# When the last weights are converted, and where copies and joins stand, at the seam between two FFNs

## The chip, the cores and the metric

The kernel runs on one core of a Trainium2 chip. Its engines are TensorE (PE in the profile; PEld is its weight load), VectorE (DVE), ScalarE (ACT), GpSimd (POOL) and SyncE (SP, which issues the DMAs). Each engine works through its own instructions in the order in which the program gives them; semaphores hold an instruction until what it needs is there. The metric is the device time of one execution in microseconds; less is better.

## The reference

Three stages run one after the other on 1536 tokens of width 512:

```
x   = attention(q, k, v)           # 16 heads, banded (|i-j| < 16) plus 24 block summaries
h   = x @ w_in                     # 512 -> 2048        first FFN
x   = (h * cos(h)) @ w_out         # 2048 -> 512
h   = x @ w_in2                    # 512 -> 1024        second FFN
e   = exp(h - max(h));  solu = h * e / (sum(e) + 1e-9)
ln  = (solu - mean) / sqrt(var + 1e-6) * g_ln
out = ln @ w_out2                  # 1024 -> 512
```

All is 32-bit in effect; the weights arrive as 64-bit floats.

## The kernel before

**Products.** A 32-bit product is made of three on PE: each operand is split into a high part (rounded by ScalarE to the format that PE takes) and a low part (the operand less its high part), and high x high, high x low and low x high are summed in PSUM (PASSES, L218). Every operand so needs a rounding and a subtraction before PE can use it.

**Weights.** The class Weights (L111) takes one block of 128 x 512 weights at a time through stages: `load` fetches the 64-bit words (tag raw, three buffers), `rebias` lets ScalarE convert both words (L164, L165), `finish` lets VectorE join them to 32-bit floats (L172, tag s, three buffers, or b, two), and for the second FFN's last weights w_out2 lets GpSimd multiply by the column g_ln (L179); `split` rounds on ScalarE (L194) and subtracts on GpSimd (L195). `turn` does one round of all stages, each for another block.

**First FFN.** 48 steps (NSTEP), each 12 products h (L245) and 12 products y (L287). `emit_chain` (L997) puts the work of the other engines for one step in order: ScalarE's u (L254), the weights' split and rebias, VectorE's n (L259), the join, gs (L274, L275), the sine (L264), r (L269). Up to four banks of y are added to X by VectorE (`evacuate`, L301). A step so converts one block of weights beside the products.

**The second FFN's first product** uses seven block products in place of eight (p = a pair of token tiles). The blocks of W and X are formed as sums: `w2_blocks` (L741) gets four blocks m1, n1, n2, m2 for each of two halves c, and forms differences of them on GpSimd (`less`, L745) and splits the seven (`w2_tile`, L735: ScalarE L737, GpSimd L738). All this is done when the block's turn comes in `split`, inside one step of the first FFN. For X, `sum_xo` (L809, GpSimd) and `split_xo` (L827) do the same for a pair.

**The seam** is written out by hand after the loop (from L1057): the last step of the first FFN, the pair 0 of the second (its products on the first FFN's spare banks), with `weights.turn()` six times for the last six blocks of w_out2, each between parts of pair 0 and pair 1. `emit_block` (L878) sums banks and takes maxima, `emit_exp2`, `emit_mult2`, `emit_stats`, `emit_factors` and `emit_scaled` make the normalised tile e; `emit_factors` ends in a power on GpSimd (L930) for which `emit_scaled` (L935) waits. Tile t = 0 is turned by PE (`turn`); later tiles by DMA: `emit_planes` (L978) separates the halves of the words, a DMA transposes them, `emit_join` (L984) puts them together on ScalarE (L991, into a buffer of tag s), rounds (L994) and subtracts on GpSimd (L995). `emit_o2` is the last product, `emit_out` copies it (L1028) and writes it.

**Loop over pairs** (L1135). For p > 1 the products m = 1, 6, 7, 5 go to four banks; m = 2 uses the bank of m = 1 again, so PE waits until ScalarE has copied it (`emit_p1`, L862), which stands behind `emit_planes(s - 2)` on ScalarE. The sums of X for the pair p + 2 take two of the three buffers s that the joins use too.

Of the kernel before, what the change touches and what calls it, by code (L numbers as in the profile page):

```python
# [34 lines left out]
def fused_kernel(  # L35
# [75 lines left out]
    class Weights:  # L111
# [5 lines left out]
        def __init__(self):  # L117
            self.jobs = []
            self.raw = {}
            self.f32 = {}  # L120
            self.done = {}
            self.next = 0
            self.queue = []
            self.ready = []
            self.limit = 0
# [15 lines left out]

        def bits(self):
# [6 lines left out]
            for n in range(i, i + 2):  # L149
                self.load(n)  # L150
            self.f32[i] = conv.tile([P, 512], I32, tag="b" if self.jobs[i][6] else "s", name="s",
                                    bufs=2 if self.jobs[i][6] else 3) if wide else self.raw[i]

        def rebias(self):

            if self.queue and wide:
                t = self.raw[self.queue[-1]]
                hw, lw = as32(t[:, :, 1]), t[:, :, 0]
                nc.scalar.activation(out=hw, in_=hw, func=AF.Prelu, scale=REBIAS, alpha=NEGATIVE)  # L164
                nc.scalar.activation(out=lw, in_=lw.bitcast(U32), func=AF.Copy, scale=TOP3)  # L165

        def finish(self):

            if self.queue and wide:
                i = self.queue[-1]  # L170
                t = self.raw[i]
                nc.vector.scalar_tensor_tensor(  # L172
                    out=self.f32[i], in0=t[:, :, 1], scalar=3, in1=t[:, :, 0],
                    op0=ALU.logical_shift_left, op1=ALU.bitwise_or)
            for i in self.queue:
                scale = self.jobs[i][4]
                if scale is not None:
                    f = as32(self.f32[i]) if wide else self.f32[i]
                    nc.gpsimd.tensor_scalar(out=f, in0=f, scalar1=scale, scalar2=None, op0=ALU.mult)  # L179
            self.ready = self.queue  # L180
            self.queue = []

        def split(self):

            for i in self.ready:
                f = self.f32.pop(i)
                f = as32(f) if wide else f
                pool, scale, then = self.jobs[i][3:6]
                if then is not None:
                    then(f)  # L190
                    self.done[i] = None
                    continue
                w = pool.tile([P, 2, 512], F32R, tag="w", name="w")
                nc.scalar.activation(out=w[:, 0, :], in_=f, func=AF.Copy)  # L194
                nc.gpsimd.tensor_tensor(out=w[:, 1, :], in0=f, in1=as32(w[:, 0, :]), op=ALU.subtract)  # L195
                self.done[i] = w
            self.ready = []
# [505 lines left out]
    with tc.manual_schedule():  # L703
# [37 lines left out]
        def w2_blocks(c):  # L741
# [4 lines left out]

            def m1(t):
# [37 lines left out]
        B_DONE, C_DONE, A_DONE = (GF * NTB * g for g in (2, 3, 4))  # L785
        ALLOWED = {B_DONE: W2O - KC, C_DONE - 2: W2O + 2, NSTEP - 3: W2O + NF2}

        def split_next(step):
# [3 lines left out]
            for p, which in XO_AT.get(step, ()):  # L792
                if 0 in which:
                    sum_xo(p)
                split_xo(p, which, nc.scalar)

# [7 lines left out]
                 NSTEP - 3: ((1, (1,)),), NSTEP - 2: ((1, (2,)),), NSTEP - 1: ((1, (3,)),)}  # L804

# [258 lines left out]
        emit_m(0, 1, 6, 7)  # L1064
        emit_u(L)
        emit_n(L)
        split_next(L)
        emit_sin(L)
        emit_r(L)
        emit_g(L)  # L1070
        emit_p1(0)
        table(AF.Exp)
        banks_of[0].append(h_tile(NSTEP + 3))
        emit_u2(0)
        emit_u3(0)
        emit_m(0, 5)
        weights.turn()
# [5 lines left out]
        weights.turn()  # L1083
# [5 lines left out]
        weights.turn()  # L1089
# [7 lines left out]
        weights.turn()  # L1097
# [11 lines left out]
        weights.turn()  # L1109
        emit_p1(1)  # L1110
        emit_u2(1)
        weights.turn()
# [22 lines left out]
        for p in range(1, NPT):  # L1135
# [18 lines left out]
            for k, o in enumerate(outs):  # L1154
                emit_o2(o, O[2 + k] if p == 1 else O[k])
# [7 lines left out]
            if p == 1:  # L1163
                emit_planes(1)
                emit_out(0)
# [4 lines left out]
            if p < NPT - 1:  # L1170
                emit_planes(f)
            emit_stats(s)
# [5 lines left out]
            if p == 1:  # L1178
                emit_join(1)
            else:  # L1180
# [57 lines left out]
```

## Time and profile before

| | |
|---|---|
| median of 3 runs | 525.38 us (524.36 to 527.4) |
| the profiled execution | 523.5 us, its span 521.7 us, mean granted clock 0.97 |
| PE busy | 478.4 us, 92% of the span |
| DVE, ACT, POOL busy | 309.3, 319.2, 239.9 us |
| chain that ended last, share by engine | PE 65%, DVE 8%, POOL 7%, ACT 6% |

The page gives the busy share of each engine in 40 slices of 13.04 us. PE is the engine with the most work; where its digit is under 9 it waits for another, and the waits view says for which. The timeline then shows what that engine was doing. A bracket at the end of a timeline row, as [3.92 <-ACT gs], is the idle time ahead of the instruction and what ended it.

### The profile page before, as it was taken

To read this page: it belongs to the slowest core of one execution; us is meant where nothing else is said; L and a number is where in the kernel's file an instruction comes from. 1 tells how busy PE (TensorE), PEld (TensorE's weight loads), DVE (VectorE), ACT (ScalarE), POOL (GpSimd) and SP (SyncE) were. 2 spreads that over 40 slices of the span, in tenths; PEclk is the share of its full clock that TensorE was granted. 3 is DMA by queue.
4 is the path that set the end of the run, shared out by engine and by line. 5 is a ranking of instruction groups with operands and counts; after the bars stand their busy time and mean duration, and the time that the engine had idled before them with its cause. 6 is when DMAs were issued, how large, how long until landed. Compare 5 with 4: busy or idle time off the path is not lost.

```text
span 521.7 us, 8063 instructions
## 1 busy us (share of the span) xinstructions
PE 478.4 (92%) x2907; PEld 390.9 (75%) x2907; DVE 309.3 (59%) x744; ACT 319.2 (61%) x566; POOL 239.9 (46%) x236
## 2 busy tenths in 40 slices
PE   8999999999999999999969969999778269999997
PEld 5777777688888888888858858888557158888886
DVE  4888576745444566465625534545687557967840
ACT  3688787747766656656544546437434377878731
POOL 3679787323221222212352255543556566785310
PEclk9999999999999999999999988999979769999999
DMA  8889854002323233232210222001200413142111
GB/s 242 254 223 221 210 141 134 1 1 93 110 82 119 82 92 111 82 109 93 84 69 8 91 70 83 0 1 40 82 1 0 101 41 91 51 103 80 42 60 42
DMA packets 59048, 46.18 MB, mean 89 GB/s; under 512 B 40448, under 2 KB 51328, under 8 KB 59008
## 3 DMA queue, kind: packets, MB, share of 16 engines
q1 hardware_dynamic: 59008, 45.67, 30.4%
q8 instruction: 23, 0.38, 0.3%
q14 instruction: 17, 0.14, 0.1%
HBM read 36.61 MB, written 3.15 MB: 76 GB/s over the span
## 4 chain that ended last, share of the span: by engine, by line
PE 65%; DVE 8%; POOL 7%; ACT 6%; issue 5%; DMA 4%; SPq 3%; POOLq 0%; DVEq 0%; ACTq 0%
PE y L287 22%; PE h L245 21%; PE h L1018 12%; PE h L854 7%; DMA vt<-in_v_dram 2%; SPq L413 2%; POOL w L738 1%; POOL s L745 1%; ACT raw L164 1%; PE sps L530 1%; DMA vt<-vm 1%; DVE s L172 1%; POOL w L195 1%; ACT raw L165 1%; POOL sm L545 1%
## 5 line engine op out<-in xcount | busy, mean ns | idle before, releaser
L287 PE MATMUL y<-gs,w 128*128 128x512 f32 x576 | 142.9, 398 | 8.4 <-ACT gs L274 7.8
L245 PE MATMUL h<-xs,w 128*128 128x512 f32 x576 | 141.3, 392 | 0.0
L287 PEld LDWEIGHTS y<-gs,w 128*128 128x128 f32 x576 | 110.6, 192 | 33.2 <-ACT gs L274 8.7
L245 PEld LDWEIGHTS h<-xs,w 128*128 128x128 f32 x576 | 107.4, 188 | 21.8
L195 POOL TENSOR_TENSOR w<-s,w 128x512 fp32r<-128x512 f32 x40 | 52.0, 1301 | 116.3 <-ACT w L194 110.7
L854 PE MATMUL h<-w,xo 128*128 128x512 f32 x252 | 62.8, 408 | 21.1 <-ACT p L862 14.2
L254 ACT ACTIVATE r<-h 128x512 int32<-128x512 f32 x48 | 28.6, 596 | 86.9 <-PE h L245 86.9
L172 DVE SCALAR_TENSOR_TENSOR s<-raw 128x512 int32<-128x512 int32 x48 | 36.8, 767 | 67.7 <-ACT raw L165 62.4
L259 DVE SCALAR_TENSOR_TENSOR r<-r,h 128x512 f32<-128x512 int32 x48 | 32.9, 686 | 73.6 <-ACT r L254 73.4
L854 PEld LDWEIGHTS h<-w,xo 128*128 128x128 f32 x252 | 49.7, 199 | 32.9 <-ACT p L862 14.6
L1018 PE MATMUL h<-w,ls 128*128 128x512 f32 (+1 forms) x312 | 67.0, 373 | 0.0
L1018 PEld LDWEIGHTS h<-w,ls 128*128 128x128 f32 x312 | 55.3, 188 | 10.2
L264 ACT ACTIVATE r<-r,half_pi 128x512 f32<-128x512 f32 x48 | 34.5, 719 | 5.1 <-DVE r L259 5.1
L269 DVE TENSOR_TENSOR h<-h,r 128x512 f32<-128x512 f32 x48 | 33.0, 688 | 5.6 <-ACT r L264 5.6
L738 POOL TENSOR_TENSOR w<-s,w 128x512 fp32r<-128x512 f32 x14 | 18.0, 1288 | 38.7 <-ACT w L737 38.7
L275 DVE TENSOR_TENSOR gs<-h,gs 128x512 fp32r<-128x512 f32 x48 | 32.7, 680 | 4.7 <-ACT gs L274 4.7
L194 ACT ACTIVATE w<-s 128x512 fp32r<-128x512 f32 x40 | 25.0, 626 | 12.4 <-POOL s L179 12.4
L164 ACT ACTIVATE raw<-raw 128x512 f32<-128x512 f32 x48 | 31.9, 665 | 0.0
L165 ACT ACTIVATE raw<-raw 128x512 int32<-128x512 uint32 x48 | 31.9, 664 | 0.0
L995 POOL TENSOR_TENSOR ls<-s,ls 128x512 fp32r<-128x512 f32 x18 | 23.3, 1293 | 17.8 <-ACT ls L994 17.8
L991 ACT ACTIVATE s<-turned 128x1024 uint16<-128x1024 uint16 x18 | 24.6, 1366 | 7.4 <-POOL xo L842 7.4
L274 ACT ACTIVATE gs<-h 128x512 fp32r<-128x512 f32 x48 | 28.2, 587 | 1.5 <-DVE h L269 1.5
(102 smaller groups left out, 671.0 us busy)
## 6 DMA issues: line engine op xcount, KB each, us to landing
raw<-in_moe_w_in_dram SPq DMA_DIRECT2D x24, 512.0 KB, 3.7
raw<-in_moe_w_out_dram SPq DMA_DIRECT2D x24, 512.0 KB, 3.5
vt<-in_v_dram SPq DMA_DIRECT2D x16, 240.0 KB, 5.7
kt<-in_k_dram SPq DMA_DIRECT2D x8, 384.0 KB, 5.2
qt<-in_q_dram SPq DMA_DIRECT2D x8, 384.0 KB, 7.1
out_dram<-osb SPq DMA_DIRECT2D x11, 256.0 KB, 2.0
vt<-vm SPq DMA_DIRECT2D x16, 72.0 KB
vt<-in_v_dram SPq DMA_DIRECT2D x16, 48.0 KB, 6.4
```

What stands on the lines that cost most here:

```text
L164: nc.scalar.activation(out=hw, in_=hw, func=AF.Prelu, scale=REBIAS, alpha=NEGATIVE)
L165: nc.scalar.activation(out=lw, in_=lw.bitcast(U32), func=AF.Copy, scale=TOP3)
L172: nc.vector.scalar_tensor_tensor(out=self.f32[i], in0=t[:, :, 1], scalar=3, in1=t[:, :, 0], op0=ALU.logical_shift_left, op1=ALU.bitwise_or)
L195: nc.gpsimd.tensor_tensor(out=w[:, 1, :], in0=f, in1=as32(w[:, 0, :]), op=ALU.subtract)
L245: nc.tensor.matmul(h, lhsT=w[:, a, f * P:(f + 1) * P], rhs=xs_of[tb, c][:, b_, :], start=(m == 0), stop=(m == 3 * KC - 1))
L259: nc.vector.scalar_tensor_tensor(out=r, in0=r.bitcast(I32), scalar=TWO_PI, in1=h_of[step], op0=ALU.mult, op1=ALU.subtract)
L264: nc.scalar.activation(out=r, in_=r, func=AF.Sin, scale=-1.0, bias=half_pi)
L269: nc.vector.tensor_tensor(out=h, in0=h, in1=r, op=ALU.mult)
L275: nc.vector.tensor_tensor(out=gs[:, 1, :], in0=r, in1=as32(gs[:, 0, :]), op=ALU.subtract)
L287: nc.tensor.matmul(y[e], lhsT=w[:, a, e * P:(e + 1) * P], rhs=gs[:, b_, :], start=(f == 0 and i == 0), stop=(f == GF - 1 and i == 2))
L854: nc.tensor.matmul(banks_of[p][BANK[m]], lhsT=x[:, a, s0:s0 + P], rhs=w2_of[m, c][:, b_, :], start=c == j == 0, stop=c == 1 and j == 2)
L1018: nc.tensor.matmul(o, lhsT=ls_of[t][f // 4][:, a, s0:s0 + P], rhs=w[:, b_, cols], start=(f == 0 and i == 0), stop=(f == NF2 - 1 and i == 2))
```

## The change

Four things are altered; the products on PE are the same and in the same order.

1. **W's sums and splits.** The split of a block that is a sum is put off to the next step (`split_later`), and one of the subtractions (n2 less n1) moves from the step of n2 to that of m2.
2. **The last product's weights.** GpSimd's multiplication by g_ln is gone: ScalarE rounds with the scale, and VectorE forms the low part as w x g less the high part (`low_one`), where GpSimd subtracted before. The stages can be called one by one; blocks 0 and 1 go through the loop some steps later than before, blocks 2 to 7 by hand, with conversion (`rebias`), join, high part and low part at separate places.
3. **X's sums** for pairs 0 and 1 are formed a step earlier.
4. **At the seam**, the second set of e products stands before u of pair 1; the first output is copied before the planes of tile 1, and uses the fourth bank instead of the third; the join of tile 1 stands before the statistics of tile 3 and so before the sums of X for pair 3.

```diff
+        def low_one(self, i):
+            f, scale = self.low.pop(i)
+            w = self.done[i]
+            nc.vector.scalar_tensor_tensor(
+                out=w[:, 1, :], in0=f, scalar=scale, in1=as32(w[:, 0, :]), op0=ALU.mult, op1=ALU.subtract)
...
-            for i in self.queue:
-                scale = self.jobs[i][4]
-                if scale is not None:
-                    f = as32(self.f32[i]) if wide else self.f32[i]
-                    nc.gpsimd.tensor_scalar(out=f, in0=f, scalar1=scale, scalar2=None, op0=ALU.mult)
...
         def split(self):
+            later, self.later = self.later, []
+            for do in later:
+                do()
...
             def n1(t):
                 f["n1"] = t
                 less("m1", "n1", "m1")
-                w2_tile((5, c), f["m1"])
+                split_later((5, "m1"))
 
             def n2(t):
                 f["n2"] = t
                 w2_tile((3, c), t)
                 less("m1", "n2", "m1")
-                w2_tile((6, c), f["m1"])
-                less("n2", "n2", "n1")
-                w2_tile((7, c), f["n2"])
+                split_later((6, "m1"))
 
             def m2(t):
                 f["m2"] = t
                 w2_tile((2, c), t)
+                less("n2", "n2", "n1")
                 less("m2", "m2", "m1")
-                w2_tile((4, c), f["m2"])
+                split_later((7, "n2"), (4, "m2"))
...
+        XO_SUM = {NSTEP - 7: 0, NSTEP - 5: 1}
+        LOAD = {NSTEP - 6: (3,), NSTEP - 5: (4,), NSTEP - 2: (5,), NSTEP - 1: (6,)}
+        REBIAS_AT = {NSTEP - 3: (2,), NSTEP - 2: (3, 4)}
+        JOIN_AT = {NSTEP - 3: (2,), NSTEP - 2: (3,)}
...
         emit_u2(0)
+        high(4)
+        rebias(5)
+        rebias(6)
         emit_u3(0)
+        low(4)
+        join(5)
+        high(5)
         emit_m(0, 5)
-        weights.turn()
...
         emit_exp2(1)
-        weights.turn()
+        join(6)
+        high(6)
+        rebias(7)
         for s in range(NSTEP - LAG, NSTEP):
             emit_y(s)
...
         emit_m(1, 1, 6, 7, 5)
-        weights.turn()
         emit_p1(1)
+        emit_mult2(1)
         emit_u2(1)
-        weights.turn()
-        assert not weights.queue and not weights.ready
+        low(5)
+        low(6)
+        join(7)
+        high(7)
         sum_xo(2)
         split_xo(2, (0, 1), nc.scalar)
-        emit_mult2(1)
         emit_u3(1)
         emit_t5(1)
         emit_block(1, 5)
+        low(7)
...
-                emit_o2(o, O[2 + k] if p == 1 else O[k])
+                emit_o2(o, O[3] if p == 1 else O[k])
...
             if p == 1:
+                emit_out(0)
                 emit_planes(1)
-                emit_out(0)
...
+            if p == 1:
+                emit_join(1)
             emit_stats(s)
             emit_factors(s)
             emit_scaled(s)
             if p + 2 < NPT:
                 sum_xo(p + 2)
                 split_xo(p + 2, (0, 1), nc.gpsimd)
-            if p == 1:
-                emit_join(1)
```

ScalarE in the two steps of the first FFN in which W's blocks n2 and m2 come (u is `r<-h`, L254 before and L286 after; a W rounding is `w<-s`, L737 and L769; gs is L274 and L306). Before:

```order
L254 ACTIVATE r<-h 128x512
L737 ACTIVATE w<-s 128x512 x3
L164 ACTIVATE raw<-raw 128x512
L165 ACTIVATE raw<-raw 128x512
L274 ACTIVATE gs<-h 128x512
L264 ACTIVATE r<-r,half_pi 128x512
L254 ACTIVATE r<-h 128x512
L737 ACTIVATE w<-s 128x512 x2
L274 ACTIVATE gs<-h 128x512
```

After, with the step behind them:

```order
L286 ACTIVATE r<-h 128x512
L769 ACTIVATE w<-s 128x512 x2
L162 ACTIVATE raw<-raw 128x512
L163 ACTIVATE raw<-raw 128x512
L306 ACTIVATE gs<-h 128x512
L296 ACTIVATE r<-r,half_pi 128x512
L286 ACTIVATE r<-h 128x512
L769 ACTIVATE w<-s 128x512 x2
L306 ACTIVATE gs<-h 128x512
L296 ACTIVATE r<-r,half_pi 128x512
L286 ACTIVATE r<-h 128x512
L769 ACTIVATE w<-s 128x512 x2
```

Six roundings of one half c, before one in the step ahead of these rows and three and two in them, now stand as two, two and two over three steps.

VectorE at the seam, from the last X sums (`X_75<-y`) to u3 of pair 1 (L873 before and L918 after); a join is `s<-raw` (L172 and L169), u is L866 and L911, the scaled e L935 and L980, the e products `e<-h,e`, the new subtraction `w<-s,gcol,w`. Before:

```order
L301 TENSOR_TENSOR X_75<-y_3539,X_75 128x512
L172 SCALAR_TENSOR_TENSOR s<-raw 128x512
L934 TENSOR_TENSOR st<-st 128x1
L935 TENSOR_SCALAR e<-e,mv,st 128x1024
L172 SCALAR_TENSOR_TENSOR s<-raw 128x512
L866 TENSOR_TENSOR u_3800<-h_3764,p_3798 128x512
L907 TENSOR_TENSOR e<-h,e 128x512 x2
L909 TENSOR_TENSOR st<-st 128x1
L873 TENSOR_TENSOR rest<-h_3765,u_3800 128x512
```

After:

```order
L333 TENSOR_TENSOR X_75<-y_3542,X_75 128x512
L979 TENSOR_TENSOR st<-st 128x1
L980 TENSOR_SCALAR e<-e,mv,st 128x1024
L952 TENSOR_TENSOR e<-h,e 128x512 x2
L954 TENSOR_TENSOR st<-st 128x1
L911 TENSOR_TENSOR u_3791<-h_3759,p_3786 128x512
L198 SCALAR_TENSOR_TENSOR w<-s,gcol,w 128x512 x2
L169 SCALAR_TENSOR_TENSOR s<-raw 128x512
L918 TENSOR_TENSOR rest<-h_3760,u_3791 128x512
```

Of two joins in this stretch one is left; it and two new subtractions stand behind u, and the second e products ahead of it. The join ahead of the first e products, which both have, is not shown.

GpSimd after the statistics of tile 2 (the power is `st<-st,mhalf`, L930 before and L975 after; X's sums are `xsum`, the low parts of a join `ls<-s,ls`). Before:

```order
L930 TENSOR_TENSOR st<-st,mhalf 128x1 x2
L817 TENSOR_TENSOR xsum<-X_74 128x256
L817 TENSOR_TENSOR xsum<-xsum,X_74 128x256
L817 TENSOR_TENSOR xsum<-X_74,xsum 128x256
L817 TENSOR_TENSOR xsum<-X_74 128x256
L841 CAST xo<-X_74 128x512
L842 TENSOR_TENSOR xo<-X_74,xo 128x512
L841 CAST xo<-xsum 128x512
L842 TENSOR_TENSOR xo<-xsum,xo 128x512
L995 TENSOR_TENSOR ls<-s,ls 128x512 x4
```

After:

```order
L975 TENSOR_TENSOR st<-st,mhalf 128x1
L1040 TENSOR_TENSOR ls<-s,ls 128x512 x2
L975 TENSOR_TENSOR st<-st,mhalf 128x1
L862 TENSOR_TENSOR xsum<-X_74 128x256
L862 TENSOR_TENSOR xsum<-xsum,X_74 128x256
```

The two low parts of the join of tile 1 have moved from behind the next pair's sums to between the powers for tile 2 and tile 3.

## Rows read from the trace of the kernel before

**Rows 1.** The page: busy tenths and granted clock in 40 slices.
```profile
PE   8999999999999999999969969999778269999997
...
DVE  4888576745444566465625534545687557967840
...
PEclk9999999999999999999999988999979769999999
```

**Rows 2.** Waits of PE, 250 to 440 us: total, times, longest.
```profile
PE y L287 <- ACT gs L274: 7.8, 2, 3.9
```

**Rows 3.** Timeline, first FFN: start and length in us, engine, line, instruction.
```profile
265.58 0.63 ACT L737 ACTIVATE w<-s 128x512 fp32r<-128x512 f32 x1 [2.64 <-POOL s L745]
...
268.83 0.63 ACT L737 ACTIVATE w<-s 128x512 fp32r<-128x512 f32 x1 [2.61 <-POOL s L745]
...
271.08 0.50 PE L287 MATMUL y<-gs,w 128*128 128x512 f32 x1 [3.92 <-ACT gs L274]
...
340.47 2.88 PE L287 MATMUL y<-gs,w 128*128 128x512 f32 x12
...
345.91 2.88 PE L287 MATMUL y<-gs,w 128*128 128x512 f32 x12
```

**Rows 4.** Windows of L254: stretch, length, busy us (count), PEclk, DMA share, GB/s.
```profile
261.50:340.40 78.90, 7.12 (x12) 0.94 0.15 51
```

**Rows 5.** Timeline of PE and DVE at the seam, 369 to 396 us.
```profile
369.03 5.60 PE L287 MATMUL y<-gs,w 128*128 128x512 f32 x24
...
369.11 0.79 DVE L172 SCALAR_TENSOR_TENSOR s<-raw 128x512 int32<-128x512 int32 x1 [1.56 <-ACT raw L165]
...
375.48 0.72 DVE L172 SCALAR_TENSOR_TENSOR s<-raw 128x512 int32<-128x512 int32 x1 [3.48 <-ACT raw L165]
...
379.31 8.08 PE L854 MATMUL h<-w,xo 128*128 128x512 f32 x24 [4.68 <-DVE X L301]
...
381.79 1.40 DVE L172 SCALAR_TENSOR_TENSOR s<-raw 128x512 int32<-128x512 int32 x1
...
383.30 1.22 DVE L935 TENSOR_SCALAR e<-e,mv,st 128x1024 f32<-128x1024 f32 x1
...
388.12 1.27 DVE L907 TENSOR_TENSOR e<-h,e 128x512 f32<-128x512 f32 x2
...
389.54 1.06 PE L962 MATMUL h<-ident,e 128*128 128x128 f32 x8 [2.15 <-DVE st L909]
...
395.19 0.69 DVE L885 CUSTOM_DVE_ANT_0 h<-h,p 128x512 f32<-128x512 f32 x1
```

**Rows 6.** Timeline at the seam, 405 to 423 us.
```profile
405.06 3.00 PE L854 MATMUL h<-w,xo 128*128 128x512 f32 x12 [2.17 <-ACT osb L1028]
...
408.03 2.00 ACT L978 ACTIVATE planes<-e 128x1024 uint16<-128x1024 uint16 x2 [3.11 <-DVE e L935]
...
410.17 0.55 POOL L930 TENSOR_TENSOR st<-st,mhalf 128x1 f32<-128x1 f32 x1 [3.79 <-DVE st L929]
...
411.46 1.30 DVE L935 TENSOR_SCALAR e<-e,mv,st 128x1024 f32<-128x1024 f32 x1
...
417.84 1.35 ACT L991 ACTIVATE s<-turned 128x1024 uint16<-128x1024 uint16 x1 [5.92 <-POOL xo L842]
...
422.29 5.76 PE L854 MATMUL h<-w,xo 128*128 128x512 f32 x18 [14.22 <-ACT p L862]
```

**Rows 7.** Groups by line and form: busy us, mean ns of one, idle before.
```profile
L259 DVE SCALAR_TENSOR_TENSOR r<-r,h 128x512 f32<-128x512 int32 x48 | 32.9, 686 | 73.6 <-ACT r L254 73.4
...
L215 DVE TENSOR_TENSOR xs<-X,xs 128x512 fp32r<-128x512 f32 x2 | 3.0, 1546 | 0.3 <-issue 0.3
...
L195 POOL TENSOR_TENSOR w<-s,w 128x512 fp32r<-128x512 f32 x40 | 52.0, 1301 | 116.3 <-ACT w L194 110.7 <-DVE ss L555 4.0 <-DVE mx L541 1.6
...
L179 POOL TENSOR_SCALAR s<-s,gcol 128x512 f32<-128x512 f32 x8 | 12.7, 1582 | 8.6 <-DVE s L172 8.0 <-DVE st L934 0.6
```

**Rows 8.** The page, DMA issues: count, median us to landing.
```profile
turned<-planes SPq DMA_TRANSPOSE x18, 2.8
```

More of the change, by code (lines that the diff above doesn't have):

```diff
@@ L124, in __init__ @@
             self.ready = []
+            self.later = []
+            self.low = {}
             self.limit = 0
@@ L148, in bits @@
             self.queue.append(i)
[L149 to L152, printed above, removed]
+            self.open(i)
         def rebias(self):
[L161 to L165, printed above, removed]
-        def finish(self):
[L169 to L174, printed above, removed]
-            for i in self.queue:
-                scale = self.jobs[i][4]
-                if scale is not None:
-                    f = as32(self.f32[i]) if wide else self.f32[i]
-                    nc.gpsimd.tensor_scalar(out=f, in0=f, scalar1=scale, scalar2=None, op0=ALU.mult)
+            if self.queue:
+                self.rebias_one(self.queue[-1])
+        def finish(self):
+            if self.queue:
+                self.join_one(self.queue[-1])
             self.ready = self.queue
@@ L183, in split @@
         def split(self):
+            later, self.later = self.later, []
+            for do in later:
+                do()
             for i in self.ready:
[L186 to L196, printed above, removed]
+                self.split_one(i)
             self.ready = []
@@ L745, in less, with split_later @@
                 nc.gpsimd.tensor_tensor(out=f[out], in0=f[x], in1=f[y], op=ALU.subtract)
+            def split_later(*blocks):
+                weights.later.append(lambda: [w2_tile((m, c), f[x]) for m, x in blocks])
             def m1(t):
@@ L784, in fused_kernel @@
         weights.limit = 3 * 2 * KC
-        B_DONE, C_DONE, A_DONE = (GF * NTB * g for g in (2, 3, 4))
-        ALLOWED = {B_DONE: W2O - KC, C_DONE - 2: W2O + 2, NSTEP - 3: W2O + NF2}
+        ALLOWED = {2 * NTB * GF: W2O - KC, 3 * NTB * GF - 2: W2O, 3 * NTB * GF + 3: W2O + 2}
         def split_next(step):
@@ L792, in split_next @@
             for p, which in XO_AT.get(step, ()):
-                if 0 in which:
-                    sum_xo(p)
                 split_xo(p, which, nc.scalar)
+            if step in XO_SUM:
+                sum_xo(XO_SUM[step])
+            for i in LOAD.get(step, ()):
+                weights.load(W2O + i)
+            for i in REBIAS_AT.get(step, ()):
+                weights.rebias_one(W2O + i)
+            for i in JOIN_AT.get(step, ()):
+                weights.open(W2O + i)
+                weights.join_one(W2O + i)
         NTT = NTOK // P
@@ L1064, in fused_kernel, with high, low, rebias @@
         emit_m(0, 1, 6, 7)
+        def high(i):
+            weights.split_one(W2O + i, True)
+        def low(i):
+            weights.low_one(W2O + i)
+        def rebias(i):
+            weights.rebias_one(W2O + i)
+        def join(i):
+            weights.open(W2O + i)
+            weights.join_one(W2O + i)
         emit_u(L)
         emit_n(L)
-        split_next(L)
+        high(2)
+        low(2)
         emit_sin(L)
         emit_r(L)
+        high(3)
         emit_g(L)
+        low(3)
+        split_next(L)
         emit_p1(0)
@@ L1073, in fused_kernel @@
         banks_of[0].append(h_tile(NSTEP + 3))
+        join(4)
+        weights.load(W2O + 7)
         emit_u2(0)
+        high(4)
+        rebias(5)
+        rebias(6)
         emit_u3(0)
+        low(4)
+        join(5)
+        high(5)
         emit_m(0, 5)
-        weights.turn()
         emit_t5(0)
@@ L1177, in fused_kernel @@
                 split_xo(p + 2, (0, 1), nc.gpsimd)
-            if p == 1:
-                emit_join(1)
-            else:
+            if p > 1:
                 emit_out(f - 2)
```

39 lines of the change are left out of this document (37 added, 2 removed).

## The prediction

> **What bounds the kernel now.** I read the slices of the page first. In [rows 1] PE is at 9 tenths in most slices, so the product engine sets the time, and a change pays only where PE stands still. It stands still in two kinds of place: two short dips (slices 20 and 23 from 0, about 261 to 274 us and 300 to 313 us), inside the loop of the first FFN, and a long ragged one (slices 28 to 32, about 365 to 430 us) at the seam. PEclk falls in the same slices, so a wait costs more than its own length.
>
> Next the waits of PE, to see who is waited for. In the loop it is ScalarE's rounding of gs, twice, 7.8 us together [rows 2]. Then the timeline around the first dip, to see what held ScalarE [rows 3]: the step in which the third block of the second W arrives has three W roundings on ScalarE (L737), and the second and third wait 2.64 and 2.61 us for a subtraction on GpSimd (L745). The rounding of gs stands behind them, and PE waits 3.92 us for it. The loss is best taken from whole steps, because it then holds the slow products as well: the windows row counts 12 steps (12 of ScalarE's L254, one per step) in 78.90 us [rows 4], while a step between two undisturbed y products (340.47 to 345.91) is 5.44 us. 78.90 - 12 x 5.44 = **13.6 us** lost in the two dips.
>
> At the seam [rows 5, 6] PE ends the last y products at 374.6 and then waits 4.68 us for VectorE's X sum, 2.15 us for VectorE's second set of e products, 2.17 us for the copy of the first output tile, and 14.22 us for ScalarE's copy p. Together 23.2 us; behind each stands a chain that the change rearranges.
>
> **The change part by part.**
>
> *W's sums a step later.* No instruction is added or removed. In a step ScalarE gets at most two W roundings, each on a sum that GpSimd formed in the step before, so none waits inside the step. GpSimd's heaviest step holds four operations of 1.3 us (L195's size, [rows 7]), 5.2 us in a step of 5.44; if the last one runs over, the next step's rounding slips by some tenths. With at most five ScalarE instructions of about 0.63 us ahead of it, gs is rounded some 3.8 us after the start of its step, and PE wants it a step after that start, so there is room. Term: **-13.6 us**. Bounds: all of it, or, if GpSimd's backlog brings one wait of 2.6 us back in each of the two places, 13.6 - 5.2 = 8.4.
>
> *Weights of the last product.* Eight times, GpSimd's scaling (1.58 us) and subtraction (1.30 us) go, 23 us of GpSimd time, and ScalarE scales while it rounds; VectorE gets eight subtractions that scale [rows 7]. The trace has none of these. Lower end: 0.69 us, what VectorE takes for the same kind of instruction with one input from PSUM (L259). Upper end: 1.55 us, for its subtraction with both inputs in SBUF beside GpSimd's (L215). All eight together are 5.5 to 12.4 us. Two stand in the loop and three at the seam ahead of the last y products; what hides them is PE, which holds queued products until 374.6, and VectorE's idle time before its waits. I cost these five at nothing, with 1.4 us (2 x 0.69, the loop's two) if that cover is gone. The last three stand on VectorE's path and are counted below.
>
> *The seam up to the first output product.* Before, VectorE reaches a join at 372.0 and waits 3.48 us for ScalarE's conversion (the join at 375.48), after another such wait of 1.56 us at 369.11. Now each conversion is issued one block of weights further ahead, so both waits go, and VectorE is there at 372.0 - 1.56 = 370.4. From that join to the end of the scaled e (383.30 + 1.22 = 384.5) it took 9.0 us, of which 1.3 is a second join that moves later: 370.4 + 7.7 = 378.1. PE resumed 3.8 us after the start of that join (379.31), so the X sum that it needs is there at 370.4 + 3.8 = 374.2, before PE is done with y at 374.6: PE goes straight on, and its 24 products take a step's 5.4 us (0.227 each) instead of 8.08, to 380.1. On VectorE follow, at 0.69 for one and 1.27 for two of 512 columns (388.12, 395.19), the second set of e products (1.4 with its small sum, to 379.5; PE's transposes need them at 380.1: no wait), u (0.7), two of the new subtractions (1.4), a join (0.75), u3 and t (1.3), a block (0.8), the third new subtraction (0.7) and the two subtractions of the turned tiles (1.3), to 386.7 with 0.1 of small gaps, and then the block that stood at 395.19: **8.5 us earlier**. PE's transposes (1.06, of which 0.8 before the next product) and 18 products (4.1) bring it from 380.1 to 385.0; the output product of 24 more, with about 0.6 of waiting for the turned tiles, ends near 391.
>
> *Contention there.* While these run, GpSimd now forms the sums and low parts of the third pair of tiles; the first of the three subtractions frees a buffer for them, and the other two and the join have both inputs in SBUF as L215 had. Each loses between 0 and 1.55 - 0.69 = 0.86 us, 0 to 2.6 together; which engine comes first is open at each, so I take half: **+1.3 us**.
>
> *Copies and the join of tile 1.* From 395.19 on VectorE's order is unchanged, so the planes of tile 2 start at 408.03 - 8.5 = 399.5. The first output copy stands ahead of the planes of tile 1, so it is there 2.0 us earlier still than the chain's shift: PE, which resumed on it at 405.06, could at 405.06 - 8.5 - 2.0 = 394.5, and with the copied bank used for the fourth product it needs it only at 391 + 18 x 0.227 = 395.1: the 2.17 us go. Then ScalarE makes planes (2.0, to 401.5), then two joins of 1.35 (417.84) and a rounding of 0.63 each, to 405.5. Before, the second of these waited 5.92 us for GpSimd to use up a buffer of the next pair's sums (417.84); those sums now come after the joins. But GpSimd's power (L930) for the next scaled e is now queued behind the two low parts of that join: the last ends at 405.5 + 1.3 = 406.8, the scaled e starts 1.3 after the power does, as before (410.17 to 411.46), at 408.1, and ends at 409.4, the planes at 411.4, and PE resumes 0.5 after them on p, at 411.9. Before it was 422.29: 10.4 us earlier, 9.1 with the contention. PE's wait for p thus stays, about 16 us long: what is late next is not the buffer but this chain of VectorE, ScalarE, GpSimd and back, and so 9 and not 23 us are won at the seam.
>
> **The sum** for the profiled execution, 523.5 us: -13.6 - 9.1 = -22.7, so 500.8. The median of the runs before is 525.38, 1.9 above that execution; the same shift gives **502.7 us**.
>
> A rule of the Trainium skill speaks against the new subtractions: "SBUF — State Buffer", section "Who interferes with whom", says that a VectorE instruction with two SBUF inputs and a GpSimd instruction that reads SBUF exclude each other, the later one waiting for the whole of the earlier. The trace agrees with it: L215 took 1.55 us on VectorE beside GpSimd's, L259 0.69 [rows 7]. By the rule every such meeting would cost in full, which is the first rival below.
>
> **The rivals.**
>
> *Full exclusion.* Every VectorE instruction with two SBUF inputs on the path from 370 to 387 (three subtractions, two joins) loses the full 0.86 us: 4.3 instead of 1.3, so 502.7 + 3.0 = 505.7. For it: the join at 381.79 took 1.40 us. Against: GpSimd has 23 us less to do, and for some of them it waits itself for their result.
>
> *The seam gives it back.* VectorE's row in [rows 1] is at 6 to 8 tenths in slices 28 to 30; if its extra work and its waits for ScalarE in order keep that chain where it was, only the loop's part is left: 525.4 - 13.6 = 511.8. Against: the waits of 3.48 and 1.56 us are ScalarE's lateness, not VectorE's load.
>
> *The loop keeps its dips*, since GpSimd's work there is the same and only moved: 525.4 - 9.1 = 516.3. Against: the wait is ScalarE's, in order, on results not yet begun.
>
> *No change at all* would need both of the last two.
>
> *Slower: the transposes hold GpSimd.* GpSimd's power now waits behind low parts which wait for ScalarE's join, and that for the transposed planes to land. They land 2.8 us after issue [rows 8]; issued at 396.4 behind an output write in one queue, they are there at 399.2, and ScalarE comes for them at 401.5. From a landing later than 5.1 us on, every microsecond is one on p and PE; to end above 528 us it must be 25 us more, 30 in all. For it: three pairs of transposes queue up with the write. Against: the median of 18 landings is a tenth of that.
>
> **How the numbers follow.** The forecast has 0.72, with its own range 499.5 to 505.5; full exclusion 0.08; the seam gives it back 0.09; the loop keeps its dips 0.04; no change 0.03; slower 0.04. The low end is undisturbed VectorE and the profiled execution's own base (523.5 - 24.0 = 499.5, and half a microsecond); the high end is the contention in full with the loop's term at its lower bound (502.7 + 1.3 + 5.2 = 509.2), which also takes in full exclusion: 499 to 509. About 0.5% (2.6 us) is what the runs can tell from no change; faster has 0.93, the same 0.03, slower 0.04.
>
> **What would show it right or wrong.** Right: no wait of PE for gs in the loop, 12 steps over the W blocks in 65 to 66 us; PE without a gap between the last y and the products that follow; a wait for p of 15 to 17 us, with L930's successor behind GpSimd's low parts; VectorE's new subtractions at 0.7 to 1.55 us. Wrong: a gs wait in the steps after those of before; a VectorE wait for the weight roundings at the seam; or PE resuming after p more than 24 us or less than 20 us earlier than at 422.29, counted from the span's start.

## The result, and the profile after

After the change the kernel takes 499.16 us (median of 4 runs, 497.83 to 503.47), before it 525.91 (4 runs, 524.36 to 527.4): a ratio of 0.951, 95% interval 0.944 to 0.957. The forecast was 502.7, the range 499 to 509. The profiled execution took 499.53 us (span 497.6, mean granted clock 0.983); before it was 523.5 us.

The page of the kernel after: busy time, then busy tenths and granted clock in 40 slices (now of 12.44 us).

```profile
PE 471.0 (95%) x2907; PEld 387.5 (78%) x2907; DVE 314.8 (63%) x752; ACT 319.5 (64%) x566; POOL 219.5 (44%) x220
...
PE   8999899999999999999999999999997099999997
...
DVE  3978775664444554746566465747999386877840
...
PEclk9999999999999999999999999999999589999999
```

Against [rows 1], the two dips of the loop are gone, and of the ragged stretch at the seam one hole is left (slices 30 and 31); PE's share of the chain that ended last has risen from 65 to 77%. The waits of PE from 240 to 500 us (total, times, longest) give it a single name:

```profile
PE h L899 <- ACT p L907: 14.4, 1, 14.4
```

The waits for gs [rows 2] and, at the seam, for X, for the e products and for the first output copy [rows 5, 6] are gone. The windows row that answers to [rows 4] (the line of u is now L286) counts 15 steps where there were 12, at full clock:

```profile
261.50:340.40 78.90, 8.96 (x15) 1.00 0.16 53
```

The timeline of PE alone, from the step that answers to the one ahead of the first dip to the first output products of pair 2 (start and length in us; the bracket is idle time ahead and what ended it):

```profile
256.76 2.88 PE L319 MATMUL y<-gs,w 128*128 128x512 f32 x12
...
343.81 2.88 PE L319 MATMUL y<-gs,w 128*128 128x512 f32 x12
...
356.05 5.60 PE L319 MATMUL y<-gs,w 128*128 128x512 f32 x24
361.49 5.61 PE L899 MATMUL h<-w,xo 128*128 128x512 f32 x24
...
367.72 4.34 PE L899 MATMUL h<-w,xo 128*128 128x512 f32 x18
...
377.34 5.60 PE L899 MATMUL h<-w,xo 128*128 128x512 f32 x24
397.35 6.59 PE L899 MATMUL h<-w,xo 128*128 128x512 f32 x18 [14.41 <-ACT p L907]
403.78 11.04 PE L1063 MATMUL h<-w,ls 128*128 128x512 f32 x48
```

From 256.76 to 343.81 are 16 steps of 5.44 us. The last y products (356.05, before 369.03) run into the next products without the gap of 4.68 us, and the 24 products behind them take 5.6 and not 8.08.

The profiled executions also differ in what comes ahead of the first FFN, which the change doesn't touch: its first 24 y products start between 99.4 and 107.4 us over the profiles of this study. So all kernels are compared by stages of the trace, from starts of PE: *first FFN* is from those products to its last 24 y products; *to p* from there to PE's first product after its wait for p of pair 2; *second FFN* from the last y products to the turning of the first of the last pair's tiles (eight transposes, before at 499.97, after at 475.87). The ratio of each kernel is to the runs of before that were made with it. One of the six runs of e10 was slow; its median is that of the other five.

| kernel | start of first FFN | first FFN | to p | second FFN | median | ratio to before, 95% |
|---|---|---|---|---|---|---|
| before | 100.95 | 268.08 | 53.26 | 130.94 | 525.9 | |
| after | 101.59 | 254.46 | 41.30 | 119.82 | 499.2 | 0.951 (0.944 to 0.957) |
| e1 loop only | 107.44 | 255.74 | 53.21 | 131.91 | 513.7 | 0.978 (0.970 to 0.986) |
| e2 seam only | 104.15 | 267.95 | 41.33 | 119.23 | 513.5 | 0.976 (0.968 to 0.983) |
| e8 weights only | 102.56 | 267.82 | 43.97 | 122.75 | 516.9 | 0.983 (0.976 to 0.990) |
| e3 join back | 102.81 | 254.46 | 43.31 | 122.76 | 503.9 | 0.956 (0.949 to 0.964) |
| e4 PE's waits back | 101.62 | 254.50 | 41.96 | 119.63 | 501.4 | 0.955 (0.949 to 0.960) |
| e5 power first | 103.05 | 254.45 | 37.28 | 115.92 | 495.5 | 0.944 (0.938 to 0.950) |
| e6 power and p first | 102.06 | 254.45 | 35.39 | 117.16 | 497.5 | 0.947 (0.940 to 0.954) |
| e7 next pair first | 99.39 | 254.49 | no such wait | 117.17 | 497.6 | 0.947 (0.941 to 0.953) |
| e9 p first once | 101.44 | 254.49 | 35.41 | 115.99 | 496.6 | 0.944 (0.939 to 0.948) |
| e10 next pair and copies | 102.19 | 254.46 | no such wait | 118.19 | 498.5 | 0.947 (0.941 to 0.953) |

After against before: -13.6 in the first FFN, -11.1 in the second, +0.6 in the start: -24.1, as in the spans (521.7 to 497.6).

### The profile page after: what moved, and what is told of

It reads as the page before. It is cut to its first block, busy times and chain, and to the rows that moved or that the text cites. A ratio compares the mean times of both kernels' runs of the same rounds, so it can differ in the third digit from the quotient of the medians.

```text
span 497.6 us, 8050 instructions
## 1 busy us (share of the span) xinstructions
PE 471.0 (95%) x2907; PEld 387.5 (78%) x2907; DVE 314.8 (63%) x752; ACT 319.5 (64%) x566; POOL 219.5 (44%) x220
## 4 chain that ended last, share of the span: by engine, by line
PE 77%; DVE 8%; ACT 4%; DMA 3%; POOL 3%; issue 2%; SPq 2%; POOLq 0%; ACTq 0%
PE y L319 25%; PE h L277 25%; PE h L1063 12%; PE h L899 9%; PE sps L562 2%; DMA vt<-in_v_dram 2%; PE vsum L473 1%; DMA qt<-in_q_dram 1%; DVE e L952 1%; PE aps L599 1%; SPq L445 1%; DVE e L980 1%; POOL sm L577 1%; POOL w L187 1%; ACT at L604 1%
## 5 line engine op out<-in xcount | busy, mean ns | idle before, releaser
L319 PE MATMUL y<-gs,w 128*128 128x512 f32 x576 | 138.2, 389 | 0.0
L319 PEld LDWEIGHTS y<-gs,w 128*128 128x128 f32 x576 | 108.0, 188 | 22.5
L187 POOL TENSOR_TENSOR w<-s,w 128x512 fp32r<-128x512 f32 x32 | 41.7, 1303 | 102.8 <-ACT w L186 95.3
L286 ACT ACTIVATE r<-h 128x512 int32<-128x512 f32 x48 | 28.6, 597 | 87.1 <-PE h L277 87.0
L899 PE MATMUL h<-w,xo 128*128 128x512 f32 x252 | 60.9, 400 | 14.4 <-ACT p L907 14.4
L899 PEld LDWEIGHTS h<-w,xo 128*128 128x128 f32 x252 | 48.8, 194 | 25.1 <-ACT p L907 14.8
L169 DVE SCALAR_TENSOR_TENSOR s<-raw 128x512 int32<-128x512 int32 x48 | 37.6, 783 | 44.6 <-ACT raw L163 43.4
L1040 POOL TENSOR_TENSOR ls<-s,ls 128x512 fp32r<-128x512 f32 x18 | 23.3, 1293 | 20.4 <-ACT ls L1039 20.4
L770 POOL TENSOR_TENSOR w<-s,w 128x512 fp32r<-128x512 f32 x14 | 17.9, 1293 | 30.8 <-ACT w L769 30.8
L306 ACT ACTIVATE gs<-h 128x512 fp32r<-128x512 f32 x48 | 28.2, 587 | 0.4 <-DVE h L301 0.4
L577 POOL TENSOR_TENSOR sm<-sm,mx 128x480 f32<-128x480 f32 x24 | 24.6, 1025 | 8.0 <-DVE mx L573 8.0
L592 POOL TENSOR_TENSOR sm<-sm,ss 128x480 f32<-128x480 f32 x24 | 26.2, 1094 | 0.3 <-ACT at L604 0.2
```

The costliest lines, as they stand in the source:

```text
L169: nc.vector.scalar_tensor_tensor(out=self.f32[i], in0=t[:, :, 1], scalar=3, in1=t[:, :, 0], op0=ALU.logical_shift_left, op1=ALU.bitwise_or)
L319: nc.tensor.matmul(y[e], lhsT=w[:, a, e * P:(e + 1) * P], rhs=gs[:, b_, :], start=(f == 0 and i == 0), stop=(f == GF - 1 and i == 2))
L899: nc.tensor.matmul(banks_of[p][BANK[m]], lhsT=x[:, a, s0:s0 + P], rhs=w2_of[m, c][:, b_, :], start=c == j == 0, stop=c == 1 and j == 2)
```

## The experiments

**e1 and e2: the two halves apart.** e1 is the kernel before with the put-off splits alone, e2 the kernel after without them.

```diff
-                w2_tile((5, c), f["m1"])
+                split_later((5, "m1"))
...
-                w2_tile((6, c), f["m1"])
-                less("n2", "n2", "n1")
-                w2_tile((7, c), f["n2"])
+                split_later((6, "m1"))
...
+                less("n2", "n2", "n1")
                 less("m2", "m2", "m1")
-                w2_tile((4, c), f["m2"])
+                split_later((7, "n2"), (4, "m2"))
```

> The kernel before with only W's sums split a step later. Theory: the two dips of the loop go and nothing else moves: 78.90 us for 12 steps become 65 to 66, the span shortens by 12 to 13.6 us, 525.9 becomes 512.3 to 514. The two first blocks of w_out2 still follow W's last block directly, so one rounding may wait there for GpSimd's scaling: up to 1.5 us of the gain may stay out. Rival (GpSimd's load sets the loop): the dips only move a step, under 5 us are won, over 520.

> The changed kernel with W's sums split at once as before. Theory: parts add up, so the changed kernel's 499.2 plus the loop's 13 to 13.6: 512 to 513. Both gs waits of 3.9 us are back. Rival (the conversion of the last weights, which was moved later, had its share in the second dip): the second dip is smaller, 509 to 511.

From PE's waits from 240 to 500 us in e1, whose waits at the seam are all there (the one for p, 14.2 us, is shown further below):

```profile
PE h L860 <- DVE X L305: 4.7, 1, 4.7
...
PE y L291 <- DVE gs L279: 0.9, 1, 0.9
```

and in e2, where those for gs are:

```profile
PE y L319 <- ACT gs L306: 7.8, 2, 3.9
```

e1 shortens the first FFN by 12.3 us and leaves "to p" at 53.2; e2 leaves the first FFN at 268 and has 41.3 to p. The halves don't touch each other but for 1.3 us: alone, the put-off splits leave PE one wait of 0.9 us for VectorE's part of gs, in a step in which ScalarE waits 0.92 us for GpSimd's scaling of a block of w_out2 (L180, at 314.70), as e1's expectation allowed for. It is not there when the weights are changed too. The medians, -13.3 and -13.4 us to the runs of before that went with them (526.94), add up to -26.7, and the change has -26.7.

**e3: the join of tile 1 back behind the sums for pair 3.**

```diff
-            if p == 1:
-                emit_join(1)
             emit_stats(s)
...
-            if p > 1:
+            if p == 1:
+                emit_join(1)
+            else:
                 emit_out(f - 2)
```

> The changed kernel with the join of tile 1 back behind the sums of X for pair 3. Theory: its second half waits again for GpSimd's fourth operation on those sums, at 394.8 us of the span, planes and p follow, PE resumes at 399.3 instead of 397.35: 499.2 + 2.0 = 501.2 (500.3 to 502). Rival (that buffer wait of 5.9 us was the price before and the move won all of it): 505.

Timeline of e3: counted from the start of the last y products, the power comes 5.0 us earlier than after's (388.46 - 357.27 = 31.2, after 392.19 - 356.05 = 36.1), but ScalarE's second part of the join waits, as in [rows 6], for GpSimd to use up a buffer of X's sums:

```profile
388.46 0.55 POOL L975 TENSOR_TENSOR st<-st,mhalf 128x1 f32<-128x1 f32 x1 [3.78 <-DVE st L974]
...
396.14 1.35 ACT L1036 ACTIVATE s<-turned 128x1024 uint16<-128x1024 uint16 x1 [5.91 <-POOL xo L887]
...
399.95 0.57 ACT L907 ACTIVATE p<-h 128x512 f32<-128x512 f32 x1
...
400.58 1.65 PE L899 MATMUL h<-w,xo 128*128 128x512 f32 x3 [16.42 <-ACT p L907]
```

To p it is 2.0 us longer than after, as the theory had it. Over the second FFN it is 2.9 longer; 0.6 of the difference lies in the 18 products behind p (7.18 us, after 6.59). The median of 503.9 lies above the theory's range. The join's move exchanges one wait of 5.9 us on ScalarE for a shorter one behind GpSimd's low parts.

**e4: the waits of PE for the e products and for the copy put back**, on the kernel after.

```diff
-        emit_mult2(1)
         emit_u2(1)
...
         split_xo(2, (0, 1), nc.scalar)
+        emit_mult2(1)
         emit_u3(1)
...
-                emit_o2(o, O[3] if p == 1 else O[k])
+                emit_o2(o, O[2 + k] if p == 1 else O[k])
...
-                emit_out(0)
                 emit_planes(1)
+                emit_out(0)
```

> The changed kernel with three orders undone: second e products behind the weights' subtractions, first output copied behind the planes of tile 1, from the third bank. Theory: PE gets waits of about 1.5 and 2 us back ahead of its long wait for p, which shrinks by as much, since p comes over VectorE, ScalarE and GpSimd: no change, 498.5 to 500. Rival (PE's waits add up): 499.2 + 3.5 = 502.7.

PE's waits in e4:

```profile
PE h L899 <- ACT p L907: 12.3, 1, 12.3
PE h L1007 <- ACT xo L884: 1.4, 1, 1.4
PE h L899 <- ACT osb L1073: 1.0, 1, 1.0
```

Two waits, 2.4 us together, are back and the one for p is 2.1 shorter. To p it is 0.7 us longer than after (41.96 and 41.30). That comes over VectorE and not over PE's waits: the block of t stands 16.9 us behind the start of the last y products where after has 16.2, mostly because the third new subtraction now meets a longer instruction of GpSimd that began before it, and takes 1.57 us (after 1.06):

```profile
370.05 1.29 POOL L887 TENSOR_TENSOR xo<-X,xo 128x512 fp32r<-128x512 f32 x1
...
370.32 1.57 DVE L198 SCALAR_TENSOR_TENSOR w<-s,gcol,w 128x512 fp32r<-128x512 f32 x1
```

So what PE waits ahead of p costs nothing by itself, but the order of the second e products is worth 0.7 us on VectorE. The second FFN is what it was (119.63 and 119.82) only since the 18 products behind p took 5.71 us and not 6.59. The median is 2.3 us above after's, over the theory's range and inside the intervals; the profiled execution, at 499.4, doesn't show that difference.

**e8: of the seam, only the weights.** The edits of e2, e3 and e4 together on the kernel after, so that of the change the new stages of the weights and the earlier X sums are left.

```diff
-                split_later((5, "m1"))
+                w2_tile((5, c), f["m1"])
...
+            if p == 1:
+                emit_join(1)
+            else:
...
+                emit_o2(o, O[2 + k] if p == 1 else O[k])
```

> The kernel before with only the last product's weights converted in separate stages (and X's sums a step earlier): W's sums at once, copy, second e products and join of tile 1 at their old places. Theory: the path of the seam runs over VectorE, and these stages alone shorten it up to the block behind the turned tiles by about 10 us; the join of tile 1 at its old place gives 2 back: 515 to 518. Rival (the reordered copies, e products and join carry the seam's gain): 520 or more.

PE's waits at the seam:

```profile
PE h L897 <- ACT p L905: 14.3, 1, 14.3
...
PE h L1005 <- ACT xo L882: 1.4, 1, 1.4
```

"To p" is 9.3 us shorter than before, the second FFN 8.2. The new stages of the weights, with X's earlier sums, so carry about three quarters of the seam's gain, and with them alone the wait of 4.7 us for X is gone. To p the parts add up: 9.3 here, 2.0 for the join of tile 1 (e3) and 0.7 for the second e products (e4) are the 12.0 of the change. No run parts the earlier conversions, GpSimd's dropped scaling and X's earlier sums from each other.

**e5: the power ahead of the join's low parts.**

```diff
-            if p == 1:
-                emit_join(1)
             emit_stats(s)
             emit_factors(s)
+            if p == 1:
+                emit_join(1)
```

> The changed kernel with the join of tile 1 behind the power for tile 3 (still ahead of the sums of X for pair 3). Theory: the power no longer waits for the join's two low parts on GpSimd; the scaled e is done at 389.8 us of the span instead of 394.8, the planes of tile 3 then start when ScalarE ends the join, 390.9, and PE resumes at 393.4 instead of 397.35: 495.2 (494.5 to 496). Rival (the power's place does not matter, ScalarE's order does): 499.2.

Timeline of e5: the power runs as soon as the statistics are there, the scaled e is ready while ScalarE still joins, and the planes and p follow the join at once.

```profile
388.68 0.55 POOL L975 TENSOR_TENSOR st<-st,mhalf 128x1 f32<-128x1 f32 x1 [3.78 <-DVE st L974]
...
389.46 0.81 DVE L980 TENSOR_SCALAR e<-e,mv,st 128x1024 f32<-128x1024 f32 x1
...
392.25 1.99 ACT L1023 ACTIVATE planes<-e 128x1024 uint16<-128x1024 uint16 x2
...
394.15 0.58 ACT L907 ACTIVATE p<-h 128x512 f32<-128x512 f32 x1
```

To p it is 4.0 us shorter than after, over the second FFN 3.9. So the power of 0.55 us, in line behind two low parts that wait for ScalarE, cost the changed kernel 4 us.

**e6 and e9: p ahead of the planes too**, in every pair (e6) and in pair 2 alone (e9, whose diff this is), both on e5.

```diff
+                if p == 2:
+                    emit_p1(p)
                 emit_planes(s - 2)
-                emit_p1(p)
+                if p > 2:
+                    emit_p1(p)
```

> As the one before, and in each pair p is copied ahead of the planes of the pair before. Theory: p follows the join of tile 1 at 390.9, PE resumes at 391.5 instead of 397.35: 493.3 (492.3 to 494.5). Rival (the planes are then late for the last product of tile 3): the gain beyond the one before is lost, 495.2.

> The changed kernel with the join of tile 1 behind the power for tile 3, and p ahead of the planes only in pair 2. In the trace of the run that had p first in every pair, PE resumed 35.4 us after the start of the last y products (41.3 in the changed kernel), but each later pair then lost about 1 us on the copy of an output tile. Theory: the first is kept and the second goes: 5 us under the changed kernel, 494. Rival (later pairs lose from the shifted planes of tile 3, not from the order in them): 495.5 or more.

PE's timeline in e9, from the wait for p on:

```profile
391.34 6.69 PE L899 MATMUL h<-w,xo 128*128 128x512 f32 x18 [8.52 <-ACT p L907]
...
411.12 4.37 PE L899 MATMUL h<-w,xo 128*128 128x512 f32 x18 [0.84 <-ACT osb L1073]
415.96 4.40 PE L899 MATMUL h<-w,xo 128*128 128x512 f32 x18 [0.47 <-ACT p L907]
```

PE resumes 1.9 us earlier than in e5 in both, and both give it back: in e9 pair 3 takes 22.3 us (408.76 to 431.08) where in the kernel after a pair takes 20.4, with two waits of 0.84 and 0.47 us for what ScalarE now does later; in e6 every later pair waits up to 0.7 us for a copy, 1.8 in all. Over the second FFN e9 equals e5, and e6 is 1.2 us worse. Both missed their theories (493.3 and 494; measured 497.5 and 496.6). e9 came out as its rival had it: pair 3 loses although the order in it is the old one.

**e7 and e10: the next pair's products ahead of the output products**, so that PE need not wait for p; on e5, and e10 with the copy of the second output moved up as well (the last hunk).

```diff
                 emit_out(0)
+                banks_of[2] = pair_banks(2)
+                emit_m(2, 1, 6, 7, 5)
+                emit_p1(2)
+                emit_u2(2)
+                emit_u3(2)
+                emit_t5(2)
                 emit_planes(1)
...
                 emit_out(f - 3)
+                if p == 2:
+                    emit_out(f - 2)
                 emit_join(s - 2, (1,))
```

> As e5, and p, u, u3 and t of pair 2 stand directly behind the first output copy and the scaled e of tile 2, ahead of the planes of tile 2, the join and the statistics of tile 3. Theory: PE waits only about 1.5 us for u, goes through the other 18 products by 388.5, and the next wait is for the low parts of tiles 1 and 2: the output products of both are through at about 405.5 instead of 414.7: 490 (487 to 494). Rival (the low parts queue up on GpSimd and the wait comes back in full there): 495.

> As the run with pair 2's p, u, u3 and t first, and the output copy of tile 2 ahead of the second half of the join of tile 3. In that run's trace PE no longer waited for p, but 2.5 us for this copy, and the 36 products behind it took 10.1 us instead of 8.2. Theory: the wait and the slow products go, the start of the output products of pair 3's turn comes 4 us earlier: 61 us after the start of the last y products instead of 65.5 (68.1 in the changed kernel), 492. Rival (the wait moves to the low parts of tile 3 on GpSimd): 495.

Both missed their theories (490 and 492 us), at 497.6 and 498.5 us. PE's timeline in e7:

```profile
383.58 3.00 PE L899 MATMUL h<-w,xo 128*128 128x512 f32 x12 [1.44 <-DVE u L911]
...
388.89 7.33 PE L1063 MATMUL h<-w,ls 128*128 128x512 f32 x24 [1.24 <-POOL ls L1040]
398.70 6.92 PE L1063 MATMUL h<-w,ls 128*128 128x512 f32 x22 [2.48 <-POOL ls L1040]
...
409.45 10.07 PE L899 MATMUL h<-w,xo 128*128 128x512 f32 x36 [2.46 <-ACT osb L1073]
```

The wait for p is gone, and in its place PE waits in four pieces, 7.6 us, for VectorE's u, GpSimd's low parts and a copy, with slow products behind the last three (24 take 7.33 us, 22 take 6.92, 36 take 10.07). In e10 the wait for the copy is gone too, but the one for GpSimd's low parts is longer and p of pair 3 takes the copy's place; the output products of pair 3's turn start 66.5 us after the last y products, where the theory had 61 and e7 65.5:

```profile
401.49 6.77 PE L1063 MATMUL h<-w,ls 128*128 128x512 f32 x22 [3.25 <-POOL ls L1040]
...
417.32 6.00 PE L899 MATMUL h<-w,xo 128*128 128x512 f32 x18 [3.57 <-ACT p L907]
```

Behind PE's hole at the seam stands the chain of the other three engines for tiles 1 to 3, which neither of these two orders of PE's products shortened. Of the versions tried, e5 and e9 are the shortest by the trace, 3.9 and 3.8 us under the changed kernel in the second FFN with the same first FFN; by the medians they are 3.7 and 2.6 us under it, but the intervals overlap.

## Why the prediction was right, and what it sized wrongly

**The loop, right to a tenth.** The term was -13.6, the first FFN is 13.6 us shorter, no wait for gs is left, and 12 steps take 65.3 us. e1 shows that the put-off splits do 12.3 of it by themselves, and e2 that nothing of it comes without them. The text read PEclk as falling in the same slices as PE; in [rows 1] it is at 9 in slices 20 and 28 and falls in 23, 24 and 29 to 32, partly behind the waits. No term hangs on that, since the loss was taken from whole steps.

**The seam, right in its mechanism, 2.9 us too small up to p.** By the text's own marks it failed narrowly: PE resumes 24.9 us earlier than at 422.29, where over 24 was to mean wrong, and waits 14.4 us for p, where 15 to 17 were named. The steps, on the path to the block of t (before at 395.19), in the timeline of VectorE and GpSimd after:

```profile
357.31 0.69 DVE L169 SCALAR_TENSOR_TENSOR s<-raw 128x512 int32<-128x512 int32 x1
...
363.78 0.81 DVE L980 TENSOR_SCALAR e<-e,mv,st 128x1024 f32<-128x1024 f32 x1
364.50 1.28 DVE L952 TENSOR_TENSOR e<-h,e 128x512 f32<-128x512 f32 x2
...
366.37 1.40 DVE L198 SCALAR_TENSOR_TENSOR w<-s,gcol,w 128x512 fp32r<-128x512 f32 x2
367.25 1.72 POOL L862 TENSOR_TENSOR xsum<-X 128x256 f32<-128x256 f32 x1 [4.08 <-DVE w L198]
...
369.87 0.74 POOL L862 TENSOR_TENSOR xsum<-X,xsum 128x256 f32<-128x256 f32 x1
...
370.10 1.06 DVE L198 SCALAR_TENSOR_TENSOR w<-s,gcol,w 128x512 fp32r<-128x512 f32 x1
...
372.29 0.68 DVE L930 CUSTOM_DVE_ANT_0 h<-h,p 128x512 f32<-128x512 f32 x1
```

- *VectorE's waits for the conversions go*: right. The join stands, without a wait ahead of it, 1.3 us behind the start of the last y products; forecast 370.4 - 369.03 = 1.4. The text doesn't name that before's path to the block ran over GpSimd further on. ScalarE waited 5.38 us for GpSimd's scaling and later 2.40 us for X's sum queued behind such work, and VectorE waited 2.67 us for ScalarE's rounding behind that. Of this, after has only 0.17 us left (ScalarE's wait for X's sum, at 369.83). Before:

```profile
385.02 0.63 ACT L194 ACTIVATE w<-s 128x512 fp32r<-128x512 f32 x1 [5.38 <-POOL s L179]
...
393.99 1.29 DVE L964 TENSOR_TENSOR ls<-h,ls 128x512 fp32r<-128x512 f32 x2 [2.67 <-ACT ls L963]
```

- *From the join to the block*: mis-sized. The block stands 16.2 us behind that start, before 26.2: 9.9 us won. The forecast was 8.5, less 1.3 for contention: 7.2. Of the 2.7 us between them, 0.6 lies ahead of the second e products, mostly because the scaled e took 0.81 us and not the 1.22 of [rows 5]. From there to the block the text added up 8.6 us, and the trace has 7.8 (364.50 to 372.29) with contention in it: it had summed printed durations (0.69), while such instructions start 0.60 to 0.61 apart when they follow each other (368.30, 368.90, 369.50 for u3, t and the next block). Without the contention the stretch is 7.5 us: 0.9 of the 1.1 between is that, and the rest is 0.1 of gaps and the text's own sum, whose terms make 8.45 with them and not 8.6.
- *Contention*: forecast +1.3, measured about +0.3; in proportion this is the term that was worst. The group of the new subtractions (minimum, median and maximum in ns) is undisturbed at its median, and of the three on the path only the third (370.10) is long:

```profile
L198 DVE SCALAR_TENSOR_TENSOR w<-s,gcol,w x8: 740/747/1064, 312.7 to 370.1; 128x512 fp32r<-128x512 f32 x8
```

  The text took it as open which engine comes first. For the first meeting it was not: GpSimd's first sum needs the buffer that the first subtraction frees, so it starts behind VectorE, and it is GpSimd that loses (1.72 us where the next such sum took 0.74), off the path. At the third subtraction GpSimd came first: its sum began at 369.87, 0.23 us ahead, and VectorE lost 0.3 us. The Trainium skill's "SBUF — State Buffer", "Who interferes with whom", says that issue order decides who is blocked; the trace agrees in both cases. Full exclusion on VectorE, the first rival (+4.3), didn't happen, but the small loss at the third subtraction was partly luck, which hung on the GpSimd instruction that it met: in e4 and e8, which have the second e products behind the first two, it met an instruction of 1.3 us and took 1.57 us, 0.8 more than undisturbed, nearly the 0.86 of the text's upper bound.
- *The join's move*: right. From the block to PE's first product after p it takes 25.1 us, before 27.1: 2.0 won, forecast 10.4 - 8.5 = 1.9; e3 gives the same 2.0 from the other side.
- *What is late next*: right. The power for tile 3 (L975, L930 before) stands behind the join's low parts, as these rows of the timeline after show, and e5 prices it at 4 us:

```profile
390.97 1.26 POOL L1040 TENSOR_TENSOR ls<-s,ls 128x512 fp32r<-128x512 f32 x1 [0.64 <-ACT ls L1039]
392.19 0.55 POOL L975 TENSOR_TENSOR st<-st,mhalf 128x1 f32<-128x1 f32 x1
...
393.48 1.30 DVE L980 TENSOR_SCALAR e<-e,mv,st 128x1024 f32<-128x1024 f32 x1
...
394.81 2.00 ACT L1023 ACTIVATE planes<-e 128x1024 uint16<-128x1024 uint16 x2 [3.92 <-DVE e L980]
...
396.72 0.58 ACT L907 ACTIVATE p<-h 128x512 f32<-128x512 f32 x1
```

- *PE's waits for the e products and the first copy*, 2.15 and 2.17 us: rightly left out of the sum. In e4, which has such waits again (1.4 and 1.0 us), the wait for p is 2.1 us shorter, and the 0.7 us lost up to p came over VectorE.

**A term that the sum didn't have.** The 18 products after the wait for p took 6.59 us where before took 5.76 [rows 6]: 0.8 us of the 12.0 won up to p is lost there, and 11.1 are left at the output products of pair 2 (403.78 - 356.05 = 47.7, before 58.9) and at the end. That loss is not the change's: e1 has before's seam and e2 has after's, with the same times to p, and there it is the other way round:

```profile
416.39 6.77 PE L860 MATMUL h<-w,xo 128*128 128x512 f32 x18 [14.23 <-ACT p L868]
...
413.43 5.98 PE L897 MATMUL h<-w,xo 128*128 128x512 f32 x18 [14.43 <-ACT p L905]
```

So the time of these products differs by about 1 us between profiled executions with the same seam. The 12.0 us up to p are the firm figure of the seam; a difference of under 1 us over the second FFN proves nothing here.

**The sum.** -13.6 and -11.1 against a forecast of -13.6 and -9.1, and +0.6 from a later start of the first FFN: 499.4 (measured 499.5) against 500.8. The medians lie 3.5 us apart: the 1.3 of the profiled executions, and the base, which the forecast put 1.9 us above the profile and which for the kernel after lies at its profile (499.16 and 499.53); with starts of the first FFN some us apart from run to run, that part was not to be had from one trace.

**The rivals.** The seam giving it back and the loop keeping its dips are excluded by e1 and e2, each of which has its own 13 us. The transposes never held GpSimd in the profiled execution: ScalarE takes up the first of tile 1 at 387.00 without a wait.

## What to carry to other kernels

Where an engine works in order, a short instruction on the path (here a power of 0.55 us) must not stand behind work that waits for a third engine; moving a join ahead won 2 us here by one wait removed and left 4 us lying by such a queue. Of several waits of one engine in a row, price only the last where its chain runs over other engines: PE's wait for p took up the 2.4 us of earlier waits that were put back. Add up a busy engine's stretch by distances between starts, not by printed durations, and where two engines hold each other up, ask at each meeting which comes first and how long that one is. For one meeting here the program's order told it; at another VectorE lost 0.3 or 0.8 us, by what it met.

## What was not expected of the hardware

How slow PE's products are after a wait did not follow the wait's length. The same 18 products took 5.76, 6.77 and 6.85 us after 14.2 to 14.3 us idle (before, e1, e8), 6.59 and 5.98 after 14.4 (the kernel after, e2), 7.18 after 16.4 (e3), 6.58 after 10.4 (e5), 5.71 after 12.3 (e4), 7.13 and 6.69 after 8.5 (e6, e9), while 18 products without a wait took 4.34 (367.72). The granted clock over them, a mean between the two levels of 1.2 and 2.4 GHz (0.5 and 1.0), was 0.74 in before and e4, 0.71 in e2, and 0.61 to 0.63 in the kernel after, e1, e5 and e9. Shortening the wait of 14.4 us to 8.5 so won back none of the slow products in these executions; what sets the moment at which the clock rises was not tried.

VectorE's scaled e, with one SBUF input of 1024 columns, took 0.81 us with GpSimd idle (363.78, 384.18) and 1.30 with GpSimd's sums beside it (393.48); the prediction had priced contention only for instructions with two SBUF inputs, and so carried the 1.22 us of [rows 5], taken beside GpSimd, over to a place where GpSimd was idle.
